# Batch ends of an attention and gated feed-forward kernel: k's norms as rows, softmax work moved into the output products, G/H on two PSUM banks

## The chip, the cores and the metric

One core of a Trainium2 chip. The metric is the device time of one execution in microseconds (us). Each kernel is run several times; medians are quoted.

A second measure is used, because it leaves out the start and the tail: in the profile, the time from the start of the **first** output product (tile `ps_o`) to the start of the **last** one. It is called the *body* below.

## The reference, cut to what matters

```python
B, N, C = 4, 6016, 256                                # d_ff = 1536
qn = q / (np.linalg.norm(q, axis=1, keepdims=True) + 1e-06)
kn = k / (np.linalg.norm(k, axis=1, keepdims=True) + 1e-06)
s = kn.transpose(0, 2, 1) @ qn / tau                  # 256 x 256 per batch
a = softmax(s)                                        # over the last axis
x = v @ a                                             # 6016 x 256 per batch
out = (sigmoid(x @ w_gate) * (x @ w_val)) @ w_out
```

The kernel does not form x. It forms G = a @ w_gate and H = a @ w_val once per batch (256 x 1536 each) and then works with v directly: sigmoid(v G) * (v H), times w_out. So there are four batches, and between one and the next the kernel must turn finished scores into the next G and H while TensorE keeps busy with the old batch.

## The kernel before

Each batch has 12 chunks `ci` of four 128-token tiles (the last of three). In each of 12 steps `f` of a chunk, TensorE makes a gate and a value product of 512 columns; ScalarE takes the sigmoid; VectorE multiplies (`hT`). The output products of the chunk before are spread over the steps, except in chunks 9 and 10 of the first three batches, where they follow in one block of 48 after the last step. PSUM is the memory that TensorE writes its products to; the program gives it out in banks, and a bank is free for the next product once ScalarE or VectorE has emptied it (an eviction). The prediction calls the steps with gate and value products the glu stage. All side work for the next batch `n` is queued by slot:

```python
at(9 * FC + 10, norms_mm, n)      # 16 one-column products: norms of q and k as columns
at(9 * FC + 11, norms_sqrt, n)    # ScalarE, with a load of the sqrt table
at(10 * FC + 1, norms_inv, n)     # VectorE: + 1e-6, reciprocal (4 columns)
at(10 * FC + 2, spread_k, n)      # TensorE: k's inverses as rows, 4 fp32 products
for j in range(CB):
    at(10 * FC + 1, copy_s, n, j) # VectorE: scores out of PSUM
at(10 * FC + 4, scale_k, n)       # VectorE: scores times k's inverses
at(10 * FC + 11, exps, n)         # ScalarE, with a load of the exp table
at(11 * FC + 0, sums, n)          # row sums; VectorE: their inverses rrow
for i in range(len(gh_order)):
    at(11 * FC + i, gh, n, i)     # 12 products for G and H, all through one bank
```

```python
def spread_k(b):
    s = st[b]
    s["rk"] = pso.tile([P, C], FP32, tag="o", name="ps_rk")
    for j in range(CB):
        mm(s["rk"][:, ds(j * P, P)],
           s["r"][:, CB + j : CB + j + 1].to_broadcast([P, P]), ident_f, True, True)

def gh(b, n, pl=None, tag=None, act=0):
    ps = (pl or psm).tile([P, FG], FP32, tag=tag or "m", name="ps_gh")
    # ... two matmuls ...
    if n % 2 == act:   # even: ScalarE empties the bank, odd: VectorE
        nc.scalar.activation(out=dst, in_=ps, func=ACT.Copy, scale=r)
    else:
        nc.vector.tensor_scalar(out=dst, in0=ps, scalar1=r, scalar2=None, op0=ALU.mult)
```

The pool `psm` has one bank, used in turn by the norms, the row sums and every G/H product. The pool `pss` has one bank, which holds the scores. Instructions keep program order on each engine.

## Time and profile before

| | before |
|---|---|
| median of three runs | 840.12 us (839.49 to 840.18) |
| span in the profile | 838.0 us |
| first / last output product starts | 56.8 / 834.1 us, a body of 777.3 us |
| one step of chunks 9 and 10 | 0.866 us: 4 products of 512 columns |
| one step of chunk 11 | 1.52 us: 4 of 384, 4 of 256, 2 of 512 columns |
| bubbles on TensorE per batch end | 0.57 + 0.24 + 0.54 + 0.30 + 0.29 = 1.94 us |

A bubble is the distance between two starts on TensorE, less what the instructions started at the first are worth in the steady stage. It must be read with one caution: some matmul records are missing from a trace. A distance that is too long by exactly 0.21 us beside a count of x1 where x2 is due is a missing record and no bubble. The chain and wait lines that carry this are in the prediction.

### The profile page before, as it was taken

The numbers are of one execution on the slowest core, as the hardware profiler recorded it, in microseconds if no ns is written. First come the engines' busy times: TensorE is split into PE (matmuls) and PEld (weight loads), VectorE is DVE, ScalarE is ACT, GpSimd is POOL, SyncE is SP. The second block draws the span as 40 slices with busy tenths as digits, with TensorE's granted clock in tenths as the row PEclk, the third lists the DMA queues.
The fourth block names the chain that finished last, engine by engine and source line by source line (L and its number), as shares of the span: only waits on it lengthen the run. The fifth ranks groups of instructions, "written<-read, shape, count | busy, mean of one in ns | idle before, by whom it ended". The sixth has DMA issues, their size and how long they took to land.

```text
span 838.0 us, 14001 instructions
## 1 busy us (share of the span) xinstructions
PE 817.0 (97%) x5338; PEld 506.6 (60%) x5338; DVE 566.3 (68%) x977; ACT 390.6 (47%) x640; POOL 83.2 (10%) x159
## 2 busy tenths in 40 slices
PE   5899999999999999999999999999999999999998
PEld 4646666665666666665565666666566556665666
DVE  2377777776667777777656777777756666666664
ACT  4554444445644444444554444444654444444442
POOL 5532100002011100000210020000000000000000
PEclk9799999999999999999999999999999999999999
DMA  9999624226655443223864453223222422322211
GB/s 209 206 205 186 124 51 89 61 51 136 125 102 107 101 102 63 54 51 85 153 132 83 92 118 80 51 73 67 60 48 51 95 51 73 78 50 65 49 36 69
DMA packets 78739, 77.18 MB, mean 92 GB/s; under 512 B 50769, under 2 KB 55633, under 8 KB 78673
## 3 DMA queue, kind: packets, MB, share of 16 engines
q0 software_dynamic: 23920, 38.81, 28.0%
q1 hardware_dynamic: 54608, 36.97, 15.8%
q8 instruction: 41, 0.67, 0.3%
q10 hardware_dynamic: 144, 0.52, 0.2%
q14 instruction: 26, 0.20, 0.1%
HBM read 78.64 MB, written 24.64 MB: 123 GB/s over the span
## 4 chain that ended last, share of the span: by engine, by line
PE 91%; DMA 3%; DVE 2%; ACT 1%; issue 1%; POOL 0%; ACTq 0%; POOLq 0%
PE ps_o L88 29%; PE ps_gate L88 28%; PE ps_val L88 28%; PE ps_s L88 4%; DMA k_sb<-in_k_dram 3%; PE ps_gh L88 2%; DVE hT L351 1%; ACT g_sb L350 1%; PE ps_rk L88 0%; DVE out_sb L377 0%; ACT gh_H L306 0%; PE ps_n L88 0%; DVE gh_H L308 0%; DVE gh_G L308 0%; DVE x_sb L253 0%
## 5 line engine op out<-in xcount | busy, mean ns | idle before, releaser
L351 DVE TENSOR_TENSOR hT<-ps_val,g_sb 128x512 bf16<-128x512 f32 (+1 forms) x576 | 391.1, 679 | 219.9 <-ACT g_sb L350 216.3
L350 ACT ACTIVATE g_sb<-ps_gate 128x512 bf16<-128x512 f32 (+1 forms) x576 | 338.8, 588 | 399.8 <-PE ps_gate L88 387.3
L88 PE MATMUL ps_val<-vT,gh_H 128*128 128x512 bf16 (+1 forms) x1152 | 338.0, 375 | 0.5
L88 PE MATMUL ps_gate<-vT,gh_G 128*128 128x512 bf16 (+1 forms) x1152 | 337.5, 375 | 0.0
L88 PE MATMUL ps_o<-w_out_sb,hT 128*128 128x256 bf16 x2256 | 326.2, 273 | 0.0
L88 PEld LDWEIGHTS <-hT 128*128 128x128 bf16 x2256 | 220.7, 98 | 124.8
L88 PEld LDWEIGHTS <-gh_H 128*128 128x128 bf16 x1152 | 112.7, 98 | 132.9 <-ACT gh_H L306 1.5
L88 PEld LDWEIGHTS <-gh_G 128*128 128x128 bf16 x1152 | 112.5, 98 | 37.4 <-ACT gh_G L306 0.3
L377 DVE COPY out_sb<-ps_o 128x256 f32<-128x256 f32 x188 | 78.1, 415 | 20.9 <-PE ps_o L88 20.9
L106 POOL DMA_DIRECT2D v_sb<-in_v_dram x48 | 25.6, 534 | 631.7 <-DMA vT<-v_sb 466.0
L88 PE MATMUL ps_s<-k_sb,q_sb 128*128 128x256 bf16 x376 | 72.4, 296 | 13.1 <-ACT k_sb L128 6.8
L88 PEld LDWEIGHTS <-q_sb 128*128 128x128 bf16 x376 | 39.1, 104 | 20.8 <-issue 7.1
L169 DVE TENSOR_TENSOR sq<-q_sb 128x1024 bf16<-128x1024 bf16 (+3 forms) x46 | 30.4, 661 | 20.7 <-PE ps_n L88 17.4
L207 DVE TENSOR_TENSOR acc<-acc,sq 128x1024 bf16<-128x1024 bf16 (+1 forms) x66 | 44.2, 669 | 0.0
L97 POOL DMA_DIRECT2D q_sb<-in_q_dram x48 | 26.4, 549 | 15.6 <-DMA q_sb<-in_q_dram 5.5
L97 POOL DMA_DIRECT2D k_sb<-in_k_dram x48 | 26.1, 545 | 13.6 <-DMA k_sb<-in_k_dram 8.4
L169 DVE TENSOR_TENSOR sq<-k_sb 128x1024 bf16<-128x1024 bf16 (+2 forms) x34 | 22.4, 658 | 0.0
L167 ACT ACTIVATE sq<-k_sb 128x1024 bf16<-128x1024 bf16 (+1 forms) x12 | 12.2, 1021 | 15.6 <-DMA k_sb<-in_k_dram 12.6
L88 PE MATMUL ps_gh<-w_gate,e_sb 128*128 128x512 bf16 x48 | 14.1, 378 | 1.6 <-DVE rrow L281 1.2
L88 PE MATMUL ps_gh<-w_val,e_sb 128*128 128x512 bf16 x48 | 14.1, 379 | 0.4
L88 PEld LDWEIGHTS <-e_sb 128*128 128x128 bf16 x112 | 9.9, 97 | 6.8 <-issue 3.2
L306 ACT ACTIVATE gh_G<-ps_gh,rrow 128x512 bf16<-128x512 f32 x12 | 8.2, 687 | 9.7 <-PE ps_gh L88 9.6
(46 smaller groups left out, 101.6 us busy)
## 6 DMA issues: line engine op xcount, KB each, us to landing
out_dram<-out_sb SPq DMA_DIRECT2D x44, 512.0 KB, 2.8
v_sb<-in_v_dram POOLq DMA_DIRECT2D x44, 256.0 KB, 3.9
q_sb<-in_q_dram POOLq DMA_DIRECT2D x43, 256.0 KB, 6.3
k_sb<-in_k_dram POOLq DMA_DIRECT2D x43, 256.0 KB, 7.8
out_dram<-out_sb SPq DMA_DIRECT2D x4, 384.0 KB, 2.4
w_gate<-in_moe_w_gate_dram POOLq DMA_DIRECT2D x3, 256.0 KB, 6.9
w_val<-in_moe_w_val_dram POOLq DMA_DIRECT2D x3, 256.0 KB, 7.6
w_out_sb<-in_moe_w_out_dram POOLq DMA_DIRECT2D x1, 768.0 KB, 12.6
```

Source lines behind the costliest of these rows:

```text
L88: nc.tensor.matmul(out, lhsT=lhsT, rhs=rhs, start=start, stop=stop, **kw)
L97: nc.gpsimd.dma_start(out=tl[:, :nt, :], in_=rows(src, b)[:, t0 : t0 + nt, :])
L106: nc.gpsimd.dma_start(out=v_sb[:, :nt, :], in_=rows(v, b)[:, t0 : t0 + nt, :])
L167: nc.scalar.activation(out=sq[:, :nt, :], in_=src[:, :nt, :], func=ACT.Square)
L169: engine.tensor_tensor(out=sq[:, :nt, :], in0=src[:, :nt, :], in1=src[:, :nt, :], op=ALU.mult)
L207: nc.vector.tensor_tensor(out=acc[:, :nt, :], in0=acc[:, :nt, :], in1=st[b]["sq", w][:, :nt, :], op=ALU.add)
L306: nc.scalar.activation(out=dst, in_=ps, func=ACT.Copy, scale=r)
L350: nc.scalar.activation(out=g_sb[:, :n], in_=ps_gate[:, :n], func=ACT.Sigmoid)
L351: nc.vector.tensor_tensor(out=hts[b, ci][:, f, :n], in0=ps_val[:, :n], in1=g_sb[:, :n], op=ALU.mult)
L377: nc.vector.tensor_copy(out=out_sb[:, s, :], in_=ps)
```

## The change

The norms of k are made directly as rows that stand in all 128 partitions, by products with an all-ones stationary operand, in one bank with q's. Root and inverses become wide (258 columns) and move, with the scalings, into the two blocks of output products, where VectorE has idle time. The scalings now read the scores in PSUM, so the two copies (`copy_s`) go. G/H products start one step later and alternate between the score bank and the old one. The head (batch 0) keeps its path.

```diff
--- before.py
+++ after.py
@@ -209,9 +209,38 @@
         )
 
     def norms_mm(b):
-        s = st[b]
-        s["n"] = psm.tile([P, 2 * CB], FP32, tag="m", name="ps_n")
-        norm_mms(s["n"], s["acc"], TPC, True, True)
+
+        s = st[b]
+        acc_q, acc_k = s["acc"]
+        ps = psm.tile([P, CB + C], FP32, tag="m", name="ps_n")
+        norm_mms(ps, (acc_q,), TPC, True, True)
+        for u in range(TPC):
+            mm(ps[:, CB:], ones_bf, acc_k[:, u, :], False, u == TPC - 1, skip_group_check=True)
+        s["n"] = ps
+
+    def wide_sqrt(b):
+        s = st[b]
+        s["n_sb"] = attp.tile([P, CB + C], FP32, tag="nsb", name="n_sb")
+        s["r"], s["rk"] = s["n_sb"][:, :CB], s["n_sb"][:, CB:]
+        nc.scalar.activation(out=s["n_sb"], in_=s["n"], func=ACT.Sqrt)
+
+    def wide_inv(b, part):
+
+        r = st[b]["n_sb"][:, (0 if part == 0 else CB + C // 2) : CB + (part + 1) * (C // 2)]
+        nc.vector.tensor_scalar(out=r, in0=r, scalar1=1e-6, scalar2=None, op0=ALU.add)
+        nc.vector.reciprocal(r, r)
+        if part == 0 and inv_tau != 1.0:
+            nc.vector.tensor_scalar(
+                out=r[:, :CB], in0=r[:, :CB], scalar1=inv_tau, scalar2=None, op0=ALU.mult
+            )
+
+    def wide_scale(b):
+        s = st[b]
+        s["x"] = attp.tile([P, CB, C], FP32, tag="x", name="x_sb")
+        for j in range(CB):
+            nc.vector.tensor_tensor(
+                out=s["x"][:, j, :], in0=s["s"][:, j, :], in1=s["rk"], op=ALU.mult
+            )
 
     def norms_sqrt(b):
         s = st[b]
@@ -419,6 +448,7 @@
 
     def side_work(b):
 
+
         side = {}
 
         def at(slot, fn, *a):
@@ -446,17 +476,18 @@
                 at(s0, acc_start, n)
             for i, (fn, w) in enumerate(((acc_square, 0), (acc_add, 0), (acc_square, 1), (acc_add, 1))):
                 at(s0 + 1 + 2 * i, fn, n, g, w)
-        at(9 * FC + 10, norms_mm, n)
-        at(9 * FC + 11, norms_sqrt, n)
-        at(10 * FC + 1, norms_inv, n)
-        at(10 * FC + 2, spread_k, n)
-        for j in range(CB):
-            at(10 * FC + 1, copy_s, n, j)
-        at(10 * FC + 4, scale_k, n)
-        at(10 * FC + 11, exps, n)
+        at(9 * FC + 9, norms_mm, n)
+        for ci, s, *call in (
+            (9, 0, wide_sqrt, n),
+            (9, 2, wide_inv, n, 0),
+            (9, 3, wide_inv, n, 1),
+            (10, 0, wide_scale, n),
+            (10, 0, exps, n),
+        ):
+            side.setdefault((ci, FC + s), []).append((call[0], call[1:]))
         at(11 * FC + 0, sums, n)
         for i in range(len(gh_order)):
-            at(11 * FC + i, gh, n, i)
+            at(11 * FC + min(i + 1, FC - 1), gh, n, i, *((pss, "s"), (psm, "m"))[i % 2])
         return side
 
 
@@ -476,6 +507,8 @@
                     gh(0, 4 + f, pso, "o", act=1)
             if prev is not None and block:
                 for s in range(TPC):
+                    for fn, a in side.get((ci, FC + s), ()):
+                        fn(*a)
                     out_mms(*prev, s * FC, (s + 1) * FC)
                     flush()
             prev = (b, ci)
```

## The prediction

> **What bounds the kernel now.** I read the page first, then the waits of TensorE over the whole run, then the timeline in order of time around the three places where one batch hands over to the next (near 200-243, 402-445 and 604-647 us), and last the same timeline for VectorE.
>
> ```profile
> PE 817.0 (97%) x5338; PEld 506.6 (60%) x5338; DVE 566.3 (68%) x977; ACT 390.6 (47%) x640; POOL 83.2 (10%) x159
> PE 91%; DMA 3%; DVE 2%; ACT 1%; issue 1%; POOL 0%; ACTq 0%; POOLq 0%
> ```
>
> The first line is busy time, the second the chain that ended last, by engine. TensorE is the bound. Because matmuls overlap, its 97% doesn't say how much is left, so I read starts instead: in the steady part a 512-column pair starts every 0.43 us (216 ns each), and 48 matmuls of 256 columns take 5.24 us (109 ns each). Any larger distance between two starts is a bubble. I went through the whole run this way. From 30 to 60 us there are some 4 us of bubbles, in the head, which the change leaves alone. From 60 us on the only repeating bubbles lie in the three batch ends. The waits of TensorE name two of the causes:
>
> ```profile
> PE ps_rk L88 <- DVE r L224: 1.2, 3, 0.4
> PE ps_gh L88 <- DVE rrow L281: 1.2, 3, 0.4
> ```
>
> (total us, times, longest.) Both occur three times, once per batch end. The timeline of TensorE at the third end shows the rest; columns are start, length, instruction, how many:
>
> ```profile
> 604.02 0.54 PE L88 MATMUL ps_n<-ones_bf,acc 128*128 128x1 bf16 x16
> 604.43 0.59 PE L88 MATMUL ps_gate<-vT,gh_G 128*128 128x512 bf16 x2
> ...
> 612.69 0.59 PE L88 MATMUL ps_val<-vT,gh_H 128*128 128x512 bf16 x2
> 613.69 0.71 PE L88 MATMUL ps_rk<-ident_f,r 128*128 128x128 f32 x4 [0.41 <-DVE r L224]
> 614.24 0.59 PE L88 MATMUL ps_gate<-vT,gh_G 128*128 128x512 bf16 x2
> ...
> 617.69 0.59 PE L88 MATMUL ps_gate<-vT,gh_G 128*128 128x512 bf16 x2
> 618.36 0.59 PE L88 MATMUL ps_val<-vT,gh_H 128*128 128x512 bf16 x2
> ...
> 628.57 0.24 PE L88 MATMUL ps_r<-ones_bf,e_sb 128*128 128x1 bf16 x4
> 629.21 0.59 PE L88 MATMUL ps_gh<-w_gate,e_sb 128*128 128x512 bf16 x2 [0.40 <-DVE rrow L281]
> ...
> 634.84 0.60 PE L88 MATMUL ps_o<-w_out_sb,hT 128*128 128x256 bf16 x4
> 635.58 0.59 PE L88 MATMUL ps_gh<-w_gate,e_sb 128*128 128x512 bf16 x2
> ...
> 644.25 0.60 PE L88 MATMUL ps_o<-w_out_sb,hT 128*128 128x256 bf16 x4
> 644.98 0.59 PE L88 MATMUL ps_gh<-w_val,e_sb 128*128 128x512 bf16 x2
> ```
>
> Subtract the steady cost from each distance. 612.69 to 613.69 is 1.00 for a pair worth 0.43: **0.57** waiting for the inverses. The four fp32 spread products then take 0.55 (613.69 to 614.24). 617.69 to 618.36: **0.24**. 628.57 to 629.21: four one-column products worth 0.10, so **0.54**, waiting until the row sums have left the bank that G/H want. 634.84 to 635.58 and 644.25 to 644.98: four output products worth 0.44, so **0.30** and **0.29**, with no releaser named; each comes just after the G/H product whose eviction VectorE made behind a copy of the output, so I read it as the single G/H bank being late. The sum is 1.94 us; the same five distances stand in the ends at 200 and 402 us within 0.01.
>
> The 0.24 has its cause on VectorE:
>
> ```profile
> 609.42 0.42 DVE L377 COPY out_sb<-ps_o 128x256 f32<-128x256 f32 x1 [0.89 <-PE ps_o L88]
> 610.73 0.42 DVE L377 COPY out_sb<-ps_o 128x256 f32<-128x256 f32 x1 [0.89 <-PE ps_o L88]
> 611.79 0.69 DVE L351 TENSOR_TENSOR hT<-ps_val,g_sb 128x512 bf16<-128x512 f32 x1 [0.64 <-ACT g_sb L350]
> ...
> 616.97 0.74 DVE L253 TENSOR_TENSOR x_sb<-x_sb,ps_rk 128x256 f32<-128x256 f32 x2
> 617.63 1.28 DVE L351 TENSOR_TENSOR hT<-ps_val,g_sb 128x512 bf16<-128x512 f32 x2
> ```
>
> The two scalings at 616.97 push the gated product back from about 617.22 to 617.63, 0.41 late; in a stage where VectorE has 0.17 us spare per 0.866 us step, 0.41 - 0.17 = 0.24 comes out on TensorE. In the blocks of output products, by contrast, VectorE idles 0.89 us before each copy. That is the place to which the change moves its work.
>
> **What the Trainium skill says.** *TensorE: Matmul & The Clock Gate*, Back-to-back issue gap, gives N/2.4 + 2.5 ns: 109 ns for 256 columns; the trace agrees (5.24 us / 48 = 109 ns). *Perfetto Trace Analysis*, Optimizing Tensor Performance, Matmuls, wants independent groups to rotate through banks so that one's evacuation lies beside the next one's products; the 0.30 and 0.29 us agree. *PSUM — Partial Sum Buffer*, The four PSUM rules, says that the first matmul of a group with its start flag clears the written-bits of the whole 2 KiB bank, so k's rows may follow q's columns in one bank without a flag of their own; the norms of before already use this, with columns only. *VectorE: DVE Perf Modes*, First, the fixed hardware budget, says the reciprocal runs as an iterative divide with a repeat count of 8. The trace has it only tiny, 178 ns for four columns and 166 for two, about 6 ns a column: far from one cycle, near the 8.3 ns that 8 cycles at the page's 0.96 GHz make.
>
> **Part by part, per batch end.**
>
> *Norms.* Before: 16 one-column products in 0.41 us, 25.6 ns each. After: 8 of these (0.205) and four of 256 columns at 109 ns (0.436), 0.64. **+0.23 us** on TensorE. All accumulators are long ready (the last addition starts at 593.8), so one step earlier brings no wait.
>
> *Spread.* The four fp32 products go: **-0.55**. The wait for inverses ahead of them: **-0.57**.
>
> *Softmax moved.* Copies, scalings and small inverse operations leave the steady glu stage: **-0.24**. In their place, in the first block: the root on 258 columns instead of 4. ScalarE has nothing else between 605.7 and 611.1 (two table loads of 1.28 us and the root); from 600 ns for 512 and 490 for 384 columns, 258 take some 0.4 us, so it ends by 607.4 and the sigmoid table is back by 608.7. Cost 0. The inverses: an addition of about 0.2 us and a reciprocal of 0.15 + 128 x 6 to 8.3 ns = 0.9 to 1.2 us, twice. Put in VectorE's order from the end of the second copy (608.53, less a small overlap): first inverse to 609.6-609.9, third copy, second inverse to 611.0-611.6, fourth copy to 611.4-612.0, and the first gated product of the next stage is due at 611.79. It is at most 0.2 late with 0.17 spare: cost 0 to 0.05. I chose 0. In the second block: two scalings of 0.41 us right behind the last gated product, from 623.3 to 624.1. The first copy goes from 623.75 to about 624.1, done by 624.5; its buffer is wanted by the third group at 622.25 + 2 x 1.31 = 624.87. The exponentials wait for the table until 623.92 anyway, when the first scaling is done. Cost 0.
>
> *G/H.* The first product waits one step and takes the freed score bank; the wait for the row sums goes (**-0.54**). With two banks each eviction has two steps of 1.52 us rather than one: **-0.59**. The last two products share a step, but the bank of the second was filled 1.95 us earlier, while the latest eviction of before needed 1.82 us from product to free bank. The next batch's scores want the score bank some 1.7 us after product 10, which ScalarE empties in about 0.7. Cost 0.
>
> Sum: 0.23 - 0.55 - 0.57 - 0.24 - 0.54 - 0.59 = **-2.26 us** per end. There are three ends (the head keeps its old path), so -6.8 us. Everything after an end is paced by TensorE, which shows no DMA wait and no repeating bubble there, so the whole of it should reach the end: 840.1 - 6.8 = 833.3, and I add 0.2 for small leftovers: **833.5 us**, 0.8% faster.
>
> **Rivals.** *The inverses become the wait.* If the reciprocal costs more per column than the small ones suggest, say 11 ns, the fourth copy ends 0.7 us later than I put it and TensorE stalls some 0.5 to 0.7 us at the start of the next stage: about 835.3. For it: nothing in the profile shows a wide reciprocal. Against: the fit from 2 to 4 columns. *The G/H bubbles stay.* If VectorE's own order, not the bank, is what holds TensorE, 0.3 to 0.6 us per end remains: 834.4 to 835.1. Against: the bubbles stand at the G/H product, not at a gate or value product. *The gain is hidden anyway.* If loads or transposes paced the stages after an end, bubbles would reappear there and the time would stay near 840. Against: TensorE's bubbles from 260 to 390 us total 0.1 us. *A larger gain* of over 2% would need 16.8 us, and all bubbles after 60 us are only some 6 us.
>
> **Range and chances.** The sum is built from measured distances that agree in all three ends, so the upper side comes from the first two rivals. Range 832.3 to 836.0. Faster by over 2%: 0.01; within 2%: 0.98; slower: 0.01.
>
> **What would show it right or wrong.** Right: no ps_rk in the batch ends; norms of about 0.64 us; no wait of ps_gh on rrow; even 1.52 us steps through G/H; the gated products after the first block on time. Wrong: a reciprocal of over 1.3 us and a late first gated product; a distance of over 0.44 us before a G/H product; a new wait of the next batch's first score; or bubbles later that give the gain back.

## The result, and the profile after

The changed kernel takes **833.66 us** (median of six runs, 832.74 to 834.39) against 839.64 us (839.29 to 840.18). The ratio is 0.9928, 95% interval 0.9916 to 0.9941: 0.7% faster. Ratios here are the mean time of one kernel's fast runs over that of the other's in the same rounds, so they are not quite the ratio of the quoted medians. The prediction was 833.5 us in a range of 832.3 to 836.0.

The page of the changed kernel, first the busy times, then the chain that ended last by engine:

```profile
PE 813.7 (98%) x5303; PEld 506.3 (61%) x5314; DVE 570.1 (69%) x977; ACT 391.1 (47%) x640; POOL 83.1 (10%) x159
PE 95%; DMA 3%; ACT 0%; POOL 0%; issue 0%; DVE 0%; POOLq 0%
```

VectorE was 2% of the chain before and ScalarE 1%; both are now 0%, and TensorE went from 91% to 95%. The waits of TensorE over the whole run (us in total, times, longest) confirm it. All three lines left belong to the head:

```profile
PE ps_s L88 <- ACT k_sb L128: 6.8, 1, 6.8
PE ps_s L88 <- DMA k_sb<-in_k_dram: 6.6, 8, 1.2
PE ps_r L88 <- ACT e_sb L288: 0.3, 1, 0.3
```

TensorE's timeline at the third batch end (start, length, instruction, how many):

```profile
599.55 0.34 PE L88 MATMUL ps_n<-ones_bf,acc 128*128 128x1 bf16 x8
599.75 0.60 PE L88 MATMUL ps_n<-acc,ones_bf 128*128 128x256 bf16 x4
600.19 0.59 PE L88 MATMUL ps_gate<-vT,gh_G 128*128 128x512 bf16 x2
...
628.07 0.59 PE L88 MATMUL ps_gh<-w_val,e_sb 128*128 128x512 bf16 x2
...
629.58 0.59 PE L88 MATMUL ps_gh<-w_val,e_sb 128*128 128x512 bf16 x2
```

The norms take 599.55 to 600.19, 0.64 us. The G/H products stand 1.51 us apart, an even step without a bubble. From the gate product of step 9 in chunk 9 to the first product of the next batch, this end took 44.63 us before (602.30 to 646.93) and 42.39 after (598.69 to 641.08): **2.24 us less per end**.

VectorE in the first block of output products (in brackets: how long the engine was idle before, and what ended that):

```profile
604.74 0.42 DVE L406 COPY out_sb<-ps_o 128x256 f32<-128x256 f32 x1 [0.89 <-PE ps_o L88]
605.08 0.22 DVE L230 TENSOR_SCALAR n_sb<-n_sb 128x130 f32<-128x130 f32 x1
605.33 0.97 DVE L231 RECIPROCAL n_sb<-n_sb 128x130 f32<-128x130 f32 x1
606.21 0.36 DVE L406 COPY out_sb<-ps_o 128x256 f32<-128x256 f32 x1
606.49 0.21 DVE L230 TENSOR_SCALAR n_sb<-n_sb 128x128 f32<-128x128 f32 x1
606.74 0.95 DVE L231 RECIPROCAL n_sb<-n_sb 128x128 f32<-128x128 f32 x1
607.61 0.36 DVE L406 COPY out_sb<-ps_o 128x256 f32<-128x256 f32 x1
608.42 0.69 DVE L380 TENSOR_TENSOR hT<-ps_val,g_sb 128x512 bf16<-128x512 f32 x1 [0.45 <-ACT g_sb L379]
```

Both inverses fit: the fourth copy ends at 607.97, and VectorE then idles 0.45 us before the first gated product.

**Where the time went, and the noise.** The body:

```profile
L88 PE MATMUL ps_o<-w_out_sb,hT x2256: 272/273/273, 57.7 to 828.2; 128*128 128x256 bf16 x188
```

828.2 - 57.7 = 770.5 us, against 777.3: a body shorter by 6.8 us, three times 2.24 within rounding. The spans differ by only 5.8 us, since in this profile the first output product came at 57.7 us rather than 56.8, before anything that the change touches. Over the thirteen profiles (before, after and eleven experiments) that first start lies anywhere from 55.4 to 57.7 us, also between kernels with the same head (57.7 and 56.8 in two profiles of the changed kernel itself). So the head is noise of up to 2.3 us, as large as several of the effects looked for below. The clock granted to TensorE differs between the thirteen profiles only in the head too: it was 0.83 to 0.94 in the first 60 us and 1.00 from 60 to 815 us in all of them, so it explains no difference between bodies.

**One thing had moved that the prediction did not mention.** Around the second block, before (ScalarE twice, then VectorE twice):

```profile
625.03 1.28 ACT L350 ACT_TABLE_LOAD   x1
628.01 0.49 ACT L350 ACTIVATE g_sb<-ps_gate 128x384 bf16<-128x384 f32 x1 [1.69 <-PE ps_gate L88]
...
628.53 0.56 DVE L351 TENSOR_TENSOR hT<-ps_val,g_sb 128x384 bf16<-128x384 f32 x1 [0.42 <-ACT g_sb L350]
629.01 0.15 DVE L281 TENSOR_SCALAR rrow<-ps_r 128x2 f32<-128x2 f32 x1
```

and after:

```profile
623.32 1.28 ACT L379 ACT_TABLE_LOAD   x1 [3.04 <-PE ps_gate L88]
624.62 0.87 ACT L379 ACTIVATE g_sb<-ps_gate 128x384 bf16<-128x384 f32 x2
...
625.14 0.56 DVE L380 TENSOR_TENSOR hT<-ps_val,g_sb 128x384 bf16<-128x384 f32 x1 [1.76 <-ACT g_sb L379]
625.62 0.15 DVE L310 TENSOR_SCALAR rrow<-ps_r 128x2 f32<-128x2 f32 x1
```

Before, the sigmoid table was loaded right behind the exponentials and was long there when the gate product came. After, ScalarE idles 3.04 us, waits for the gate product and only then loads the table. The first sigmoid of chunk 11, its gated product and, behind that in VectorE's order, the inverses of the row sums are all late by the load. The trace names the gate product as what the load waited for. Compiling the kernels shows where that wait stands in ScalarE's list of instructions (other columns cut; a wait in brackets of its own is an instruction of its own):

```
before:  Activation e_sb x2               [wait DVE]      LoadActFuncSet  Activation g_sb [waits PE]
after:   Activation e_sb [waits DVE] x2   [wait PE]       LoadActFuncSet  Activation g_sb [waits ACT]
e9:      Activation e_sb [waits DVE] x2   LoadActFuncSet  [wait PE]       Activation g_sb [waits ACT]
```

The sigmoid has two things to wait for, and one of the two waits stands as an instruction of its own ahead of the table load. Before, that was the wait for VectorE, which was long over; after, it is the wait for the gate product. A likely reason for the exchange is that the exponentials now wait for VectorE themselves, so that the sigmoid need not; this is a reading of the list and was not tested. (e9 is the experiment below in which the load is written out by hand.) The late load cost the changed kernel nothing, but the experiments show that this was no matter of course.

### The profile page after: what moved, and what is told of

The parts are those of the page before. It is cut to its first block, busy times and chain, and to the rows that moved or that the text cites. A ratio compares the mean times of both kernels' runs of the same rounds, so it can differ in the third digit from the quotient of the medians.

```text
span 832.2 us, 13944 instructions
## 1 busy us (share of the span) xinstructions
PE 813.7 (98%) x5303; PEld 506.3 (61%) x5314; DVE 570.1 (69%) x977; ACT 391.1 (47%) x640; POOL 83.1 (10%) x159
## 4 chain that ended last, share of the span: by engine, by line
PE 95%; DMA 3%; ACT 0%; POOL 0%; issue 0%; DVE 0%; POOLq 0%
PE ps_o L88 30%; PE ps_val L88 29%; PE ps_gate L88 29%; PE ps_s L88 4%; DMA k_sb<-in_k_dram 3%; PE ps_gh L88 2%; PE ps_n L88 0%; ACT gh_H L335 0%; PE ps_busy L88 0%; ACT e_sb L288 0%; POOL q_sb L97 0%; PE ps_rk L88 0%; PE ps_tp L352 0%; POOL k_sb L97 0%; PE ps_r L88 0%
## 5 line engine op out<-in xcount | busy, mean ns | idle before, releaser
L379 ACT ACT_TABLE_LOAD x6 | 7.7, 1283 | 9.2 <-PE ps_gate L88 9.1
```

The lines of the kernel that those rows point to most:

```text
L379: nc.scalar.activation(out=g_sb[:, :n], in_=ps_gate[:, :n], func=ACT.Sigmoid)
```

## The experiments

Ten further kernels and one repeat of the changed one, all correct. "Body" is from the profile; the ratio is to the kernel before in the same rounds.

| kernel | ratio, 95% interval | first / last output product | body, us | body expected |
|---|---|---|---|---|
| before | 1 | 56.8 / 834.1 | 777.3 | |
| changed | 0.9928 (0.9916 to 0.9941) | 57.7 / 828.2 | 770.5 | 770.5 (by the predicted 6.8) |
| e1_softmax_only | 1.0009 (0.9993 to 1.0024) | 57.6 / 835.5 | 777.9 | 773.9 |
| e2_gh_only | 0.9959 (0.9942 to 0.9976) | 55.4 / 829.3 | 773.9 | 773.9 |
| e3_banks_no_shift | 0.9931 (0.9916 to 0.9946) | 56.8 / 828.4 | 771.6 | 770.5 |
| e4_shift_one_bank | 0.9988 (0.9973 to 1.0004) | 57.5 / 834.1 | 776.6 | 774.1 to 775.0 |
| e5_inverse_in_steady | 0.9974 (0.9956 to 0.9992) | 55.5 / 831.2 | 775.7 | 776.6 |
| e6_double_inverse | 0.9961 (0.9945 to 0.9978) | 55.7 / 830.1 | 774.4 | 774.1 |
| e7_spread_in_block | 0.9927 (0.9910 to 0.9944) | 57.7 / 828.8 | 771.1 | 771.5 |
| after_again | 0.9923 (0.9908 to 0.9938) | 56.8 / 827.3 | 770.5 | 770.5 |
| e9_softmax_only_early_load | 0.9964 (0.9951 to 0.9978) | 56.0 / 830.1 | 774.1 | 773.9 |
| e10_no_shift_early_load | 0.9922 (0.9906 to 0.9937) | 55.4 / 825.9 | 770.5 | 770.5 |
| e8_fold | 0.9903 (0.9888 to 0.9918) | 55.5 / 824.6 | 769.1 | 769.1 |

### The two halves alone: e1_softmax_only and e2_gh_only

e1 is the changed kernel with G/H as before:

```diff
-at(11 * FC + min(i + 1, FC - 1), gh, n, i, *((pss, "s"), (psm, "m"))[i % 2])
+at(11 * FC + i, gh, n, i)
```

> The softmax half of the change alone (k's norms as rows, inverses and scalings in the blocks of output products); G/H as before on one bank. If the terms add as predicted, it gains 0.57 + 0.55 + 0.24 - 0.23 = 1.13 us per batch end, 3.4 us of the 6.8: ratio near 0.996, first to last output product 773.9 us (777.3 before, 770.5 with the whole change). In the profile no ps_rk in the ends, but the wait of ps_gh on rrow (0.54) and the two 0.30 us bubbles still there. Rival, that the halves overlap and the waits of one hide behind the other's: 770.5 or 777.3.

Measured: no gain at all, a body of 777.9 us, and a ratio of 1.0009. The waits of TensorE in it:

```profile
PE ps_gh L88 <- DVE rrow L310: 5.2, 3, 1.7
```

The waits for `r`, the spread products and the 0.24 us are gone, as expected, but the wait for the row sums' inverses, 0.54 us of bubble per end before, is now 1.88 us (628.68 to 630.66 in the third end, less 0.10 for four one-column products). 1.88 - 0.54 = 1.34 us eats the 1.13 us that the half gains. The expectation of e1 failed here, and neither it nor its rival had foreseen it.

e2 is the reverse: the kernel before with only that G/H line exchanged.

> The G/H half alone (two banks, one step later); softmax as before. Terms as predicted: 0.54 + 0.59 = 1.13 us per end, 3.4 us in all, ratio near 0.996, first to last output product 773.9 us. The waits on r, the spread products and the 0.24 us bubble stay; no bubble before a G/H product. Rival, that the bubbles before G/H products come from VectorE's order and not from the bank: 0.3 to 0.6 us per end remain, 774.8 to 775.7.

Measured: 773.9 us, as expected to the tenth. The bubbles of 0.57 and 0.25 us stay in the profile, and no bubble stands before a G/H product. That rules out the rival by which VectorE's order alone held those products. (e2 has the second bank and the delay at once; e4, e9 and e10 below part the two.)

So one half gives 3.4 us, the other -0.6, and both together 6.8. The halves are not additive.

### What ate the first half: e9_softmax_only_early_load

e1 with the table load made explicit, where it can wait for nothing:

```diff
             (10, 0, exps, n),
+            (10, 0, nc.scalar.preload_act_table, ACT.Sigmoid),
```

> The softmax half alone gained nothing, against 3.4 us expected: its profile has a bubble of 1.88 us per end before the first G/H product, waiting for the inverse of the row sums. The reading: the load of the sigmoid table now waits for the gate product, 1.28 us late, because the exponentials before it have already waited for VectorE; sigmoid, gated product and, behind that in VectorE's order, the row sums are late with it. This is the same half with an explicit load of the sigmoid table right after the exponentials. If the reading holds, the wait falls from 1.88 to 0.54 us as before, the half gains its 1.13 us per end: 773.9 us from first to last output product (777.9 without, 777.3 before). Rival, that the wide scalings or the exponentials themselves are what is late: 777.9 us, the wait stays.

Measured: 774.1 us, 3.8 less than e1, by one moved load. The wait line of e1 becomes

```profile
PE ps_gh L88 <- DVE rrow L310: 1.4, 3, 0.5
```

which is nearly that of the kernel before (1.2 in total). In the third end the load now starts at 620.98 us, right behind the exponentials, and waits for nothing. The late table load is the cause, and the rival (scalings or exponentials late) falls: those were left as they were.

### Which part of the G/H half is needed: e3_banks_no_shift, e4_shift_one_bank, e10_no_shift_early_load

e3 keeps two banks but drops the delay of one step (`at(11 * FC + i, gh, n, i, *((pss, "s"), (psm, "m"))[i % 2])`).

> The whole change, but G/H product i stays in step i on the two banks: the first one follows the row sums at once. If it is the bank that the first product waited for (the row sums had to leave it), the other bank is free and nothing is lost: 770.5 us as with the whole change, possibly a short wait of the second G/H product. Rival, that it waits for the inverse of the row sums as such: 0.54 us per end comes back, 772.1 us.

Measured: 771.6 us. The first G/H product no longer waits; the second, which takes the row sums' bank, has a bubble of 0.36 us per end:

```profile
PE ps_gh L88 <- DVE rrow L310: 0.6, 3, 0.2
```

e10 is e3 with the same early load of the sigmoid table as in e9.

> Two banks, G/H product i still in step i, with the early load of the sigmoid table. Without it this kernel had a bubble of 0.36 us per end before the second G/H product, which waited for the row sums' inverse to be read out of its bank. If that bubble too came from the late table, it goes and the time from first to last output product is that of the whole change, 770.5 us (771.6 without): the step of delay would then only be a guard against the late table. Rival, that the second product waits for the row sums anyway: 771.6 us.

Measured: 770.5 us, and no wait of ps_gh is listed. e10 differs from e9 only in the second bank, and the wait of 0.5 us that e9 still has is gone. So what the first product waited for before was the bank, and the delay of one step is only needed against the late table load.

e4 keeps the delay and drops the second bank (`at(11 * FC + min(i + 1, FC - 1), gh, n, i)`).

> The whole change, but G/H on one bank, still one step later. If one bank is the limit: the wait on the row sums is gone, but a bubble of about 0.3 us stands where VectorE's eviction falls behind a copy of the output (once or twice per end), and the last product, which shares a step with the one before, waits for its eviction, about 0.9 us: 1.2 to 1.5 us per end, 774.1 to 775.0 us. Rival, that one step more is all that was needed: 770.5 us.

Measured: 776.6 us, worse than expected. The two wait lines that are new:

```profile
PE ps_gh L88 <- ACT gh_H L335: 2.3, 3, 0.8
PE ps_gh L88 <- DVE rrow L310: 1.9, 3, 0.6
```

By starts, the bubbles per end are 0.94 us before the last product, 0.29 us at one product (both as expected) and 0.78 us before the first, which had not been: by the wait line, the delay of one step does not suffice against the late table when the first product needs the row sums' bank (e4 with an early load was not run). The 0.29 us stands where VectorE's eviction (638.29 in the third end) falls behind a copy of the output (637.96), and with two banks it is gone. That was an inference in the prediction; here it is seen.

### Is it the place of VectorE's work? e5_inverse_in_steady, e6_double_inverse

e5 puts the two wide inverses into the steady stage, where the small one stood:

```diff
-            (9, 2, wide_inv, n, 0),
-            (9, 3, wide_inv, n, 1),
+        at(10 * FC + 1, wide_inv, n, 0)
+        at(10 * FC + 1, wide_inv, n, 1)
```

> The whole change, but the two wide inverses run in the second step of the glu stage after the first block, where the small inverse stood before. They take VectorE about 2.2 us there (0.22 + 0.90 twice by the starts in the profile of the changed kernel). With 0.17 us spare per step, TensorE should lose about 2.2 - 0.17 = 2.0 us per end: first to last output product 776.6 us, nearly the time of before. Rival, that TensorE runs far enough ahead to hide it: 770.5 us.

Measured: 775.7 us, with a new wait:

```profile
PE ps_val L88 <- DVE hT L380: 4.7, 3, 1.6
```

The bubble by starts is 1.74 us per end, not 2.0. The expectation took off one slack of 0.17 us and there are two. VectorE's work takes 2.2 us (611.12 to 613.33 in the third end). About 0.25 of it lies in time before the next gated product is due: in the steady stage the next thing could start 0.61 us after a gated product, and the next gated product comes after 0.866. TensorE then runs some 0.17 us further before it needs the buffer: a value product starts 0.89 us after the gated product that frees its buffer when nothing is late, and 0.73 us after it at the bubble of 0.24 us in the kernel before (0.68 in e5). 2.2 - 0.25 - 0.17 = 1.78. The bubble of 0.24 us before obeys the same sum: the two scalings hold VectorE 0.66 us from start to start, and 0.66 - 0.25 - 0.17 = 0.24.

e6 makes each reciprocal twice, in place:

```diff
+        spare = attp.tile([P, CB + C // 2], FP32, tag="spare", name="spare")
+        nc.vector.reciprocal(spare[:, : r.shape[-1]], r)
```

> The whole change with each reciprocal made twice (the second result thrown away), in place: some 0.9 us more of VectorE's time, twice, in the first block. In the changed kernel the fourth copy ends 0.45 us before the next gated product is due, and a step has 0.17 spare. So 1.8 - 0.45 - 0.17 = 1.2 us of bubble per end right after the first block: 774.1 us. Rival, that the slack of the block is larger than this reading (the copies may wait without harm): 770.5 to 771.5 us.

Measured: 774.4 us, a bubble of 1.30 us per end for 1.2 expected, right after the first block and named as a wait of ps_val for VectorE. The two added reciprocals took 1.97 us by their starts rather than 1.8, so the slack of the block is 1.97 - 1.30 = 0.67 us, near the 0.62 that its timeline shows (0.45 + 0.17), and the rival of a larger slack falls.

### Rows by ones products, or just the place? e7_spread_in_block

The norms and the spread of before, placed in the blocks, with the changed G/H:

```diff
+            (9, 0, norms_sqrt, n),
+            (9, 2, norms_inv, n),
+            (9, 2, copy_s, n, 0),
+            (9, 3, copy_s, n, 1),
+            (9, 3, spread_k, n),      # into psm's bank
+            (10, 0, scale_k, n),
+            (10, 0, exps, n),
```

> Before's norms and its spread by four fp32 products, but the small inverses, copies, spread and scalings placed in the blocks, and G/H as in the changed kernel. If the place is what pays and not the rows, all waits are gone, and only the difference of the TensorE work is left: 0.55 - 0.23 = 0.32 us per end, 771.5 us. Rival, that the spread still makes TensorE wait for VectorE in the block: over 772.5 us, with a wait of ps_rk named.

Measured: 771.1 us, only 0.6 us above the changed kernel and with no wait of ps_rk. Inside the block the four fp32 products cost 0.44 us (606.02 to 606.46), not the 0.55 they took right after a bubble, and the old norms 0.40 rather than 0.64. So the rows themselves are worth 0.2 us per end, and the place is worth the rest of the softmax half's 1.13.

### Head and repeat: after_again

> The changed kernel once more, to see the head. First to last output product 770.5 us again, within 0.1. The 0.7 us that the gain fell short of the predicted 6.8 lay before the first output product (it began at 57.7 us rather than 56.8), in code the change does not touch. If that is chance, the start of the first output product varies by some 0.5 to 1 us between profiles of all kernels and the ratio lands between 0.991 and 0.994; if it is a property of the changed program, it is at 57.7 again and kernels with before's softmax are at 56.8.

Measured: 770.5 us again, with the first output product at 56.8 us, and kernels with before's softmax at 55.4 (e2) and 57.7 (e7). The start is chance, as the first branch said, though it varies by 2.3 us and not by 0.5 to 1.

### A try at beating both: e8_fold

GpSimd has spare time, so it folds the four token groups of the sums of squares into one before TensorE sees them:

```diff
+    def fold(b):
+        for acc in st[b]["acc"]:
+            for h in (TPC // 2, TPC // 4):
+                nc.gpsimd.tensor_tensor(
+                    out=acc[:, :h, :], in0=acc[:, :h, :], in1=acc[:, h : 2 * h, :], op=ALU.add)
...
-        norm_mms(ps, (acc_q,), TPC, True, True)
-        for u in range(TPC):
-            mm(ps[:, CB:], ones_bf, acc_k[:, u, :], False, u == TPC - 1, skip_group_check=True)
+        norm_mms(ps, (acc_q,), 1, True, True)
+        mm(ps[:, CB:], ones_bf, acc_k[:, 0, :], False, True, skip_group_check=True)
...
+        at(9 * FC - 1, fold, n)
```

> A try at beating both: the whole change, with the four token groups of each sum of squares folded into one by GpSimd (two additions each, bf16) before the norms, so that TensorE makes 2 products of one column and 1 of 256 instead of 8 and 4: 0.05 + 0.11 = 0.16 us instead of 0.64. Gain 0.48 us per end, 1.4 us in all: 769.1 us from first to last output product, ratio to before near 0.9905. Rival: GpSimd's additions slow VectorE or come late for the norms, and TensorE waits: 770.5 us or more.

Measured: a body of 769.1 us, 1.4 less than the changed kernel and as expected; 831.47 us (median) against 838.99 in the same rounds. The fold on GpSimd, and the norms on TensorE, in the third end:

```profile
587.72 1.90 POOL L214 TENSOR_TENSOR acc<-acc 128x512 bf16<-128x512 bf16 x2 [3.41 <-DVE acc L207]
```

```profile
596.39 0.19 PE L88 MATMUL ps_n<-ones_bf,acc 128*128 128x1 bf16 x2
596.44 0.27 PE L88 MATMUL ps_n<-acc,ones_bf 128*128 128x256 bf16 x1
596.55 0.59 PE L88 MATMUL ps_gate<-vT,gh_G 128*128 128x512 bf16 x2
```

The norms are 0.16 us rather than 0.64, and the fold ends some 6.8 us before they need it. VectorE's gated products beside the fold keep their 0.69 us, so the rival falls. By ratios the intervals of e8 and of the changed kernel just overlap (0.9888 to 0.9918 against 0.9916 to 0.9941, from different rounds). In the same rounds e10, whose body is that of the changed kernel, took 832.87 us (832.04 to 833.57) against 831.47 (830.59 to 832.67). That e8 is the faster rests on the body, which repeated within 0.1 us in after_again and e10.

## Why the prediction was right

- **The bound and the method.** The predicted saving was 2.26 us per end and 6.8 in all; measured were 2.24 and 6.8 in the body. The total came out at 833.66 us for 833.5, and that nearness is in part luck: the medians fell by 6.0 us (839.64 to 833.66) where 6.6 had been forecast from a first median of 840.12, and the head alone varies by 2.3. The formula that the prediction quotes from the Trainium skill, N/2.4 + 2.5 ns, is given there for an isolated product and not for a stream; the stream here agrees with it all the same (last section), and the sums rest on the measured distances.
- **Norms, +0.23.** Confirmed: 0.64 us for 0.41.
- **Spread, -0.55 and -0.57.** Both gone. As work in a full pipeline the spread is worth 0.44 (e7), so a part of the 0.55 belonged to the wait ahead of it. The sum does not change.
- **Softmax moved, -0.24.** Confirmed, with cause: e5 brings such a bubble back, 1.74 us, by moving work to the old place. The inverses were predicted at the cheap end of 6 to 8.3 ns a column with a first gated product up to 0.2 us late; the slope was 6.3 and the copy was done 0.45 us early. (That VectorE idles 0.89 us before each copy holds for three of the four; before the first it is 0.42.) Rival 1 (11 ns a column) fell, and e6 shows what it would have done.
- **G/H, -0.54 and -0.59.** Confirmed alone in e2. That the bank was the cause is shown by e10 against e9 (first product), and by e4 against the changed kernel (a bubble of 0.29 with one bank, none with two). Rival 2 fell.
- **The hidden gain.** Rival 3 fell: no bubble came back later.

**What the prediction lacked** is in its step "softmax moved". It followed the sigmoid table after the root in the first block, but not after the exponentials in the second, where it counted the cost as 0. The load there started only with the gate product and put its 1.28 us in front of the sigmoid. The cost was 0 only because the G/H half had taken the row sums off TensorE's way; without that half it is 1.34 us per end, and the sum over parts, right for the whole, was wrong for the softmax half alone (3.4 us expected, -0.6 measured).

## What to carry to other kernels

When an engine is full, read the distances between starts, price each bubble against the steady cost, and find for each the buffer or engine behind it; here such a sum held to 0.1 us for the whole change, though not for one half of it. Here a bubble was the delay less two slacks, that of the delaying engine before the product is due and that of the waiting engine until it needs the buffer (0.24 us in the kernel before, 1.74 in e5). And after moving work, look at where table loads land: a change in who waits for whom can put a load behind a wait, and parts of a change that hide each other's costs can look additive until one is tried alone.

## What the Trainium skill lacked or had wrong

- *ScalarE: Activation LUTs*, Step-by-step: what each stage is for, says that a load comes right before the activation that needs it. It does not say that a wait of that activation can stand ahead of the load: here ScalarE idled 3.04 us until the gate product came, and the load's 1.28 us followed. (*Perfetto Trace Analysis*, Identifying Dependency Chains, has a part of it: an instruction that waits for several engines may have a wait instruction put before it. It says nothing of table loads.) This is 1.34 us of bubble per batch end in e1, and e9 removes it with an explicit early load.
- The same page, What ACT_TABLE_LOAD costs, puts a switch at 1283 ns plus a drain of some 1380 ns. These traces agree with the 1.28 us and show no such drain: in the changed kernel the load starts at 623.32 and the activation behind it at 624.62. Nor does a drain show ahead of a load: before the root, the load starts at 602.30, 0.02 us after the sigmoid in front of it ended (601.68 + 0.60).
- *VectorE: DVE Perf Modes*, First, the fixed hardware budget, gives a repeat count of 8 for the reciprocal, from which the prediction took 8.3 ns a column as its upper case; what a column costs, no page states. Measured in the changed kernel and the kernel before: 0.966 us for 130 columns and 0.178 for 4, that is 0.788 / 126 = 6.3 ns a column, about 6 cycles at the page's 0.96 GHz.
- *TensorE: Matmul & The Clock Gate*, Back-to-back issue gap, from which the prediction took its formula, puts a sustained stream of weight loads and products at about 131 ns for one of 512 columns. The stream in these traces takes 216 ns (a pair every 0.43 us), which is what the page's formula for an isolated product gives.
